# Second block of an attention and mixture-of-experts kernel: where on SyncE's queue a visit's stores of w1's sums stand

## The chip, the core and the metric

One Trainium2 chip, one NeuronCore. The metric is the time of one execution in device microseconds, lower is better. TensorE (PE) multiplies, VectorE (DVE), ScalarE (ACT) and GpSimd (POOL) work on elements, SyncE (SP) issues most of the transfers between HBM and SBUF. Each engine takes its instructions in program order and waits on semaphores for what the others make.

## The reference

Attention by random features for 4 batches of 8 heads (576 positions, 64 wide, 128 features), then a dense mixture of four experts over the 2304 rows that it gives:

```python
def phi(x):
    h = x @ omega.T - sum(x * x) / 2
    return exp(h - max(h)) / sqrt(m)
kv = phi(k).T @ v;  z = sum(phi(k))
x = (phi(q) @ kv) / (phi(q) @ z + 1e-6)          # 2304 x 512
p = domain_probs / domain_probs.sum(-1)
for e in range(4):                               # w1[e] 512 x 1024, w2[e] 1024 x 512
    out += p[:, e:e+1] * (relu(x @ w1[e]) @ w2[e])
```

## The kernel before

Every float32 operand of a matmul is split into a high and a low part of the type fp32r (`split`: ACT writes the high part at line 553, POOL mostly the low one at line 556), and a product is three matmuls. The rows are worked off in blocks. A *visit* is one block with one half of one expert's hidden layer. Visits 0 to N0-1 use plain products. The second block (u = 1, 768 rows) has eight visits, called visit 1 to visit 8 below, and the third (u = 2, 1024 rows) eight more. Both use a fast scheme with seven products of sums of the parts of x and of w1. For each visit, `sides` makes the parts and sums of w1: for each of two halves i (called half 0 and half 1) four tiles, `w1ah` and `w1al` (384 KB each) and `w1sh` and `w1sl` (512 KB each). There are two buffers of each of the four, so half 0 of the next visit goes to the buffer that half 0 of this visit holds. The second block makes the tiles; `keep_sides` also stores them to HBM (`kept`, line 661, eight transfers a visit on SP's queue), and the third block fetches them from there on POOL's queue.

In a visit `fast` writes the order out by hand. g is the half of w1 that a product uses, so `p1(0)` is product 1 with half 0. `keep` copies a product from PSUM to SBUF on ACT (line 928), `both` adds a product and a kept one on DVE (line 934), then relu on ACT (line 943) and the low part on DVE (line 947). Product 7 adds to the same PSUM bank that product 6 left (`start=False`), so `p7(1)` follows ACT's copy in `p6(1)`. `prepare()` stands four times in a visit of the second block (behind `p1(0)`, `p5(0)`, `p7(0)` and `p4(0)`), and each time splits one tile of w2 and then issues one load of w2 (line 549). There are three raw buffers (`w2r`), and a load takes the one that was just split, so the load behind the first split of a visit brings what the fourth split of the same visit reads. The other three bring tiles for the next visit. In the text they are load a, b, c and d. Behind `p6(1)`, `next(ready)` begins the next visit's `sides` with the split of w1 into `w1ah` and `w1al`; its steps end in the outputs, and each of its two `summed` steps issues one load of w1 (`w1r`). `begun(t)` begins an output tile (lines 744 to 746) with the first two hidden tiles. Loads of attention's k, q and v stand between visits.

```python
        p4(0)
        ...
        prepare()                  # fourth split of w2, load d
        ...
        p6(1)                      # product, then ACT's copy out of PSUM
        if v + 1 != DEEP[0]:
            next(ready, None)      # next visit: w1ah, w1al of half 0
        begun(0)
        p7(1)                      # adds to p6(1)'s bank
        begun(1)
        p3(1)
        p4(1)
        next(more, None)
        begun(2)
```

Of the kernel before, what the change touches and what calls it, by code (L numbers as in the profile page):

```python
# [6 lines left out]
F32 = mybir.dt.float32  # L7
# [7 lines left out]
def attention_moe(ctx, tc, kT, qT, kd, qd, kn, qn, vn, omT, probs, w1, w2, out):  # L15
# [10 lines left out]
    nc = tc.nc  # L26
# [4 lines left out]
    E, FP, P, _ = w1.shape  # L31
# [13 lines left out]
    scratch = ctx.enter_context(tc.tile_pool(name="scratch", bufs=1, space=bass.MemoryType.DRAM))  # L45
# [23 lines left out]
    def f32(ap):  # L69
        return ap.bitcast(F32)  # L70
# [32 lines left out]
    H = 2 * P  # L103
# [415 lines left out]
    def visit(u, n, c0, m):  # L519
        return (u, *HALVES[n], c0, m)  # L520

    BIG = {1: (START, 6 * P), 2: (START + 6 * P, 8 * P)}
    visits = [visit(0, n, 0, 2 * P) for n in range(3)]
# [63 lines left out]
    def split_w2():  # L587
        if not later_w2:
            return
        v, c = later_w2.pop(0)  # L590
        W[v, "w2", c] = a, b = pair_of(("w2h", 512), ("w2l", 512))
        split(raw.pop((v, "w2", c)), a, b, nc.scalar, nc.gpsimd)
        load("w2")
# [57 lines left out]

    made, kept = {}, {}

    def keep_sides(v):

        for i in range(2):
            kept[visits[v][1:3], i] = ts_ = tuple(
                scratch.tile([P, w * H], F32, tag=f"s{visits[v][1:3]}{i}{x}{w}", name="kept", bufs=1) for w in (3, 4) for x in "hl"
            )
            for k, t in zip(ts_, made.pop((v, i))):  # L660
                nc.sync.dma_start(k, f32(t))

    def sides(v):

# [218 lines left out]
    def fast(v):  # L883

        u, _, _, _, n = visits[v]
# [18 lines left out]
        def prepare():  # L904
            if deep:
                for _ in range(steps2.pop(0)):
                    next(ready2, None)
            else:
                split_w2()
# [4 lines left out]
        def product(g, p, where, start=True):  # L914
            if start:
                P_[g][where] = bank("g1")[:, :n]
            ps = P_[g][where]
            (wa, wc), (xa, xc) = W[v, "w1", g][p], X[p]
            for k in range(2):
                w = slice(k * P, (k + 1) * P)  # L920
                for a, x, at in ((wa, xa, 0), (wa, xc, 1), (wc, xa, 2)):
                    nc.tensor.matmul(  # L922
                        ps, a[:, w], x[:, k], start=(start and k + at == 0), stop=(k == 1 and at == 2), skip_group_check=not start
                    )

        def keep(g, where, name):
            P_[g][name] = t = held([P, 512], "sum", F32)[:, :n]
            nc.scalar.activation(t, P_[g][where], AF.Copy)  # L928
# [23 lines left out]
        def p1(g):  # L952
            product(g, 1, "u")
            keep(g, "u", "p1")
# [7 lines left out]
        def p5(g):  # L962
            product(g, 5, "b5")
            keep(g, "b5", "p5")
# [9 lines left out]
        def p4(g):  # L974
            product(g, 4, "u", start=False)
            ha, hc = (x[:, :n] for x in hs[2 * g + 1])
            nc.scalar.activation(ha, P_[g]["u"], AF.Relu)
            if deep and g == 0:
                nc.scalar.activation(r11[:, 1], P_[0]["u"], AF.Relu)
            nc.vector.scalar_tensor_tensor(hc, P_[g]["u"], 0.0, f32(ha), ALU.max, ALU.subtract)  # L980

        def p3(g):
            product(g, 3, "b5", start=False)
            both(g, 0, 1, "b5", "u2")
# [14 lines left out]
        def sevens():  # L999
# [88 lines left out]
                gathered(v, t)  # L1088
            yield 1

        p1(0)
        prepare()
        p2(0)
        if deep:
            prepare()
        p5(0)
        next(more, None)
        prepare()
# [18 lines left out]
            if v > DEEP[0] and v + 1 in DEEP:  # L1117
                start_sides2(v + 1)
        p3(0)
        if u == 1:  # L1120
            keep_sides(v)
        p4(0)
        if deep:
            less(t1[:, 1], P_[0]["p5"], r11[:, 1])
# [242 lines left out]
    def emit():  # L1367
        pairs, g1 = begin()
        later = [Halves(b, hp) for b in range(1, B) for hp in range(NP)]
        windows = {  # L1370
            0: (first_rest(pairs, opening(later[0], both=True)), 15 / 11),
            3: (joint_ticks(later[:-NP]), 76 / 45.4),
            N0: (chain(opening(later[-NP]), later_ticks(later[-NP:])), 54 / (NV * (BIG[1][1] // P + 1) * 0.8)),
        }
        ticks, n, done, per = iter(()), 0, 0.0, 0
        for v in range(len(visits)):
            if v in windows:
                for _ in ticks:
                    pass
                ticks, per = windows[v]  # L1380
                n, done = 0, 0.0
            for share in first_visit(g1) if v == 0 else fast(v) if v >= N0 else plain(v):
                done += share
                while n < done * per:
                    next(ticks, None)
                    n += 1
        store(0)
# [61 lines left out]
```

## Time and profile before

| | |
|---|---|
| median of 3 runs | 888.4 us (886.48 to 890.8) |
| the profiled execution | 886.87 us, its span 885.1 us |
| PE busy | 878.3 us, 99% of the span |
| granted TensorE clock | 1.000 of full speed, mean over the span |
| DVE, ACT, POOL busy | 586.4, 469.1, 564.7 us |
| SP's hardware queue | 102.95 MB, 35.2% of 16 engines' span |
| second block, visits 1 to 8 | from 283.7 us to about 566 us of the span |

The profile is of one execution. A busy PE is one with a matmul in flight; the waits that it lists are those in which nothing was in flight. The idle time of an engine other than PE costs nothing by itself.

### The profile page before, as it was taken

The numbers are of one execution on the slowest core, as the hardware profiler recorded it, in microseconds if no ns is written. First come the engines' busy times: TensorE is split into PE (matmuls) and PEld (weight loads), VectorE is DVE, ScalarE is ACT, GpSimd is POOL, SyncE is SP. The second block draws the span as 40 slices with busy tenths as digits, with TensorE's granted clock in tenths as the row PEclk, the third lists the DMA queues.
The fourth block names the chain that finished last, engine by engine and source line by source line (L and its number), as shares of the span: only waits on it lengthen the run. The fifth ranks groups of instructions, "written<-read, shape, count | busy, mean of one in ns | idle before, by whom it ended". The sixth has DMA issues, their size and how long they took to land.

```text
span 885.1 us, 14800 instructions
## 1 busy us (share of the span) xinstructions
PE 878.3 (99%) x5484; PEld 788.6 (89%) x5484; DVE 586.4 (66%) x1025; ACT 469.1 (53%) x1039; POOL 564.7 (64%) x494
## 2 busy tenths in 40 slices
PE   9999999999999999999999999999999999999998
PEld 9988888989888898988988899898989898998988
DVE  5755566666667646577675666975848476675847
ACT  6554677776774564555555544634443525444342
POOL 6656465555644455444454436779898888989874
PEclk9999999999999999999999999999999999999999
DMA  7664355434521856635466253834152442415132
GB/s 185 164 229 152 111 161 176 128 137 139 184 72 48 296 171 220 230 131 202 131 221 220 78 202 129 303 105 168 47 179 85 151 153 77 156 60 179 48 132 96
DMA packets 64552, 134.01 MB, mean 151 GB/s; under 512 B 10624, under 2 KB 21056, under 8 KB 64480
## 3 DMA queue, kind: packets, MB, share of 16 engines
q1 hardware_dynamic: 54512, 102.95, 35.2%
q0 software_dynamic: 9360, 29.82, 10.3%
q8 instruction: 43, 0.70, 0.3%
q10 hardware_dynamic: 608, 0.30, 0.1%
q14 instruction: 29, 0.24, 0.1%
HBM read 98.96 MB, written 34.08 MB: 150 GB/s over the span
## 4 chain that ended last, share of the span: by engine, by line
PE 89%; POOL 4%; DVE 2%; DMA 2%; issue 2%; ACT 1%; SPq 0%; POOLq 0%; ACTq 0%
PE g L922 26%; PE g L997 16%; PE g L744 8%; PE g L746 8%; PE g L745 8%; PE g L729 3%; PE g L730 3%; PE g L731 3%; PE kv L317 2%; PE k_ps L266 1%; PE q_ps L266 1%; PE qt_ps L328 1%; DMA kept<-w1ah 1%; PE q_ps L147 1%; PE kv L177 1%
## 5 line engine op out<-in xcount | busy, mean ns | idle before, releaser
L556 POOL TENSOR_TENSOR w2l<-w2r,w2h 128x512 fp32r<-128x512 f32 x93 | 123.8, 1337 | 85.4 <-ACT w2h L553 73.2
L773 DVE SCALAR_TENSOR_TENSOR acc<-g,pr,acc 128x256 f32<-128x256 f32 (+1 forms) x278 | 139.3, 539 | 37.7 <-PE g L746 27.8
L556 POOL TENSOR_TENSOR w1sl<-w1r,w1sh 128x512 fp32r<-128x512 f32 (+1 forms) x43 | 75.1, 1747 | 65.5 <-ACT w1sh L553 54.6
L744 PE MATMUL g<-w2h,hh 128*128 128x512 f32 x280 | 111.9, 400 | 1.5 <-DVE sum L934 1.3
L746 PE MATMUL g<-w2h,hl 128*128 128x512 f32 x280 | 109.7, 392 | 0.0
L745 PE MATMUL g<-w2l,hh 128*128 128x512 f32 x280 | 109.5, 391 | 0.0
L947 DVE SCALAR_TENSOR_TENSOR hl<-sum,hh 128x384 fp32r<-128x384 f32 (+1 forms) x64 | 46.8, 734 | 81.9 <-ACT hh L943 66.6
L934 DVE TENSOR_TENSOR sum<-g,sum 128x384 f32<-128x384 f32 (+1 forms) x96 | 59.3, 620 | 62.2 <-PE g L922 56.1
L922 PE MATMUL g<-xbh,w1sh 128*128 128x384 f32 (+1 forms) x256 | 93.1, 364 | 0.1
L922 PE MATMUL g<-xbl,w1sh 128*128 128x384 f32 (+1 forms) x256 | 92.9, 363 | 0.0
L922 PE MATMUL g<-xbh,w1sl 128*128 128x384 f32 (+1 forms) x256 | 92.6, 362 | 0.0
L556 POOL TENSOR_TENSOR w1al<-w1r,w1ah 128x512 fp32r<-128x512 f32 (+1 forms) x45 | 51.4, 1157 | 51.7 <-ACT w1ah L553 32.3
L928 ACT ACTIVATE sum<-g 128x384 f32<-128x384 f32 (+1 forms) x96 | 50.8, 540 | 51.5 <-PE g L922 50.4
L553 ACT ACTIVATE w2h<-w2r 128x512 fp32r<-128x512 f32 x90 | 55.3, 627 | 29.2 <-DMA w2r<-in_w 24.4
L922 PE MATMUL g<-xbh,w1ah 128*128 128x384 f32 (+1 forms) x192 | 70.1, 365 | 0.0
L922 PE MATMUL g<-xbl,w1ah 128*128 128x384 f32 (+1 forms) x192 | 69.6, 362 | 0.0
L922 PE MATMUL g<-xbh,w1al 128*128 128x384 f32 (+1 forms) x192 | 69.5, 362 | 0.0
L744 PEld LDWEIGHTS g<-w2h,hh 128*128 128x128 f32 x280 | 52.6, 188 | 12.2 <-DVE sum L934 1.6
L746 PEld LDWEIGHTS g<-w2h,hl 128*128 128x128 f32 x280 | 52.5, 188 | 11.8 <-DVE hl L980 0.5
L745 PEld LDWEIGHTS g<-w2l,hh 128*128 128x128 f32 x280 | 52.6, 188 | 9.0
L943 ACT ACTIVATE hh<-sum 128x384 fp32r<-128x384 f32 (+1 forms) x64 | 35.0, 549 | 42.3 <-DVE sum L934 41.9
L922 PEld LDWEIGHTS g<-xbh,w1sh 128*128 128x128 f32 x256 | 48.1, 188 | 6.2 <-DVE sum L934 0.6
(212 smaller groups left out, 2420.5 us busy)
## 6 DMA issues: line engine op xcount, KB each, us to landing
w2r<-in_w SPq DMA_DIRECT2D x108, 256.0 KB, 2.8
w1r<-in_w SPq DMA_DIRECT2D x38, 512.0 KB, 3.6
kept<-w1sh SPq DMA_DIRECT2D x16, 512.0 KB, 4.9
kept<-w1sl SPq DMA_DIRECT2D x16, 512.0 KB, 5.4
w1sh<-kept POOLq DMA_DIRECT2D x16, 512.0 KB, 6.0
w1sl<-kept POOLq DMA_DIRECT2D x16, 512.0 KB, 6.7
kept<-w1ah SPq DMA_DIRECT2D x16, 384.0 KB, 4.9
kept<-w1al SPq DMA_DIRECT2D x16, 384.0 KB, 4.9
```

Of the source, the lines that this page charges most:

```text
L553: hi.activation(a, t, AF.Copy)
L556: lo.tensor_tensor(c, t, f32(a), ALU.subtract)
L744: nc.tensor.matmul(ps, ha[:, ts_], wa, start=(c == 0), stop=False)
L745: nc.tensor.matmul(ps, ha[:, ts_], wc, start=False, stop=False)
L746: nc.tensor.matmul(ps, hc[:, ts_], wa, start=False, stop=(c == FH - 1))
L773: nc.vector.scalar_tensor_tensor(to, ps, sc, to, ALU.mult, ALU.add)
L922: nc.tensor.matmul(ps, a[:, w], x[:, k], start=(start and k + at == 0), stop=(k == 1 and at == 2), skip_group_check=not start)
L928: nc.scalar.activation(t, P_[g][where], AF.Copy)
L934: nc.vector.tensor_tensor(t, P_[g][where], t, ALU.add)
L943: nc.scalar.activation(ha, t, AF.Relu)
L947: nc.vector.scalar_tensor_tensor(x, y, 0.0, f32(z), ALU.max, ALU.subtract)
L997: nc.tensor.matmul(to, x, w, start=(start and f + k == 0), stop=(f + k == 3), skip_group_check=not start)
```

## The change

`keep_sides` takes the half as an argument, and is called twice in a visit of the second block: for half 0 in front of `p1(0)`, so its four stores stand on SP in front of load a, and for half 1 behind `p2(0)`, between load a and load b. Before, all eight stores stood behind `p3(0)`, between load c and load d. No transfer is added or taken away, and no other engine's instructions change their order.

```diff
-    def keep_sides(v):
-
-        for i in range(2):
-            kept[visits[v][1:3], i] = ts_ = tuple(
-                scratch.tile([P, w * H], F32, tag=f"s{visits[v][1:3]}{i}{x}{w}", name="kept", bufs=1) for w in (3, 4) for x in "hl"
-            )
-            for k, t in zip(ts_, made.pop((v, i))):
-                nc.sync.dma_start(k, f32(t))
+    def keep_sides(v, i):
+
+        kept[visits[v][1:3], i] = ts_ = tuple(
+            scratch.tile([P, w * H], F32, tag=f"s{visits[v][1:3]}{i}{x}{w}", name="kept", bufs=1) for w in (3, 4) for x in "hl"
+        )
+        for k, t in zip(ts_, made.pop((v, i))):
+            nc.sync.dma_start(k, f32(t))
...
+        if u == 1:
+            keep_sides(v, 0)
         p1(0)
         prepare()
         p2(0)
         if deep:
             prepare()
+        else:
+            keep_sides(v, 1)
         p5(0)
...
         p3(0)
-        if u == 1:
-            keep_sides(v)
         p4(0)
```

## Rows read from the trace of the kernel before

**Rows 1.** The page: busy time of the engines, the granted clock.
```profile
PE 878.3 (99%) x5484; PEld 788.6 (89%) x5484; DVE 586.4 (66%) x1025; ACT 469.1 (53%) x1039; POOL 564.7 (64%) x494
...
PEclk9999999999999999999999999999999999999999
```

**Rows 2.** Waits of PE: us in total, times, longest us.
```profile
PE g L744 <- DVE sum L934: 1.3, 1, 1.3
...
PE g L744 <- ACT kp L299: 0.2, 1, 0.2
```

**Rows 3.** Waits of all engines: those on the stores of `w1ah`.
```profile
ACT w1ah L553 <- DMA kept<-w1ah: 17.4, 9, 3.4
```

**Rows 4.** The chain in order of time, visit 6: start us, us, what.
```profile
476.09 4.86 DMA kept<-w1ah
...
481.05 0.94 ACT w1ah L553 x2
...
482.44 1.35 DVE hl L947
...
484.31 0.50 PE g L744
```

**Rows 5.** Timeline of SP, 364.6 to 372.5, visit 3: start us, us.
```profile
364.78 0.42 SPq L661 DMA_DIRECT2D kept<-w1ah  x1
...
371.14 1.12 SPq L661 DMA_DIRECT2D kept<-w1sl  x1
372.35 1.05 SPq L549 DMA_DIRECT2D w2r<-in_w  x1
```

**Rows 6.** The eight stores of rows 5 alone.
```profile
DMA to landing us min/median/max: 3.5/4.9/5.4
```

**Rows 7.** The load of rows 5, issued at 372.35, alone.
```profile
DMA to landing us min/median/max: 4.8/4.8/4.8
```

**Rows 8.** Timeline of SP, 288 to 291, visit 1.
```profile
288.13 0.34 SPq L549 DMA_DIRECT2D w1r<-in_w  x1
288.52 1.42 SPq L792 DMA_DIRECT2D out<-acc  x2
290.10 0.37 SPq L549 DMA_DIRECT2D w2r<-in_w  x1
```

**Rows 9.** The load of w2 issued at 290.10 alone.
```profile
DMA to landing us min/median/max: 4.1/4.1/4.1
```

**Rows 10.** Timelines of ACT and PE, visit 1.
```profile
295.20 0.62 ACT L553 ACTIVATE w2h<-w2r 128x512 fp32r<-128x512 f32 x1
295.72 0.48 ACT L928 ACTIVATE sum<-g 128x384 f32<-128x384 f32 x1
...
296.52 0.34 PE L922 MATMUL g<-xbh,w1sh 128*128 128x384 f32 x1
```

**Rows 11.** Timelines of SP, ACT and PE, visit 4.
```profile
394.98 0.33 SPq L549 DMA_DIRECT2D w2r<-in_w  x1
...
402.97 0.49 ACT L928 ACTIVATE sum<-g 128x384 f32<-128x384 f32 x1
...
404.10 0.33 PE L922 MATMUL g<-xbh,w1sh 128*128 128x384 f32 x1
```

**Rows 12.** The load of w2 issued at 394.98 alone.
```profile
DMA to landing us min/median/max: 4.0/4.0/4.0
```

**Rows 13.** Timelines of SP and PE, visit 2.
```profile
318.05 0.33 SPq L549 DMA_DIRECT2D w1r<-in_w  x1
...
329.29 0.33 PE L922 MATMUL g<-xbh,w1sh 128*128 128x384 f32 x1
```

**Rows 14.** The load of w1 issued at 318.05 alone.
```profile
DMA to landing us min/median/max: 3.5/3.5/3.5
```

**Rows 15.** Timeline of POOL, 547 to 556, visit 8.
```profile
548.97 0.73 POOL L606 TENSOR_TENSOR va<-w2r 128x256 f32<-128x256 f32 x1 [0.46 <-DMA w2r<-in_w]
...
554.15 2.35 POOL L556 TENSOR_TENSOR w2s<-va,w2s 128x512 fp32r<-128x512 f32 x1 [1.81 <-ACT w2s L553]
```

**Rows 16.** The eight stores of visit 1 alone, issued from 295.6 to 303.
```profile
DMA to landing us min/median/max: 3.4/5.9/6.3
```

## The prediction, made before the change was run

> **What bounds the kernel now.** I read the page first. TensorE is busy in 99% of the span, at its full granted clock (2.4 GHz) in all 40 slices, and no other engine is above two thirds [rows 1]. So a wait counts only if TensorE stands still for it. The list of TensorE's own waits says how much of that there is: one wait of 1.3 us on VectorE's sum and one of 0.2 us on ScalarE's kp are the only ones in the second block [rows 2]. The list over all engines then shows what the stores cost today: ScalarE waits 17.4 us in nine waits, the longest 3.4 us, before it may overwrite `w1ah`, because the store out of that buffer has not landed [rows 3]. The chain in order of time ties one of these waits to TensorE. In visit 6 the store of `w1ah` takes 4.9 us, ScalarE's split follows at 481.05, its relu is queued behind, then VectorE's low part, then its sum, and the output matmul at 484.31 is the one that lost 1.3 us [rows 2, 4]. The shorter one, in visit 3, stands behind such a wait too. So of 17.4 us of waiting TensorE felt 1.5 us.
>
> **What the change takes away.** Half 0 is stored in front of `p1(0)`, nine products earlier, and needs no new producer: its tiles were split during the visit before. At `next(ready)` its stores have then landed, and ScalarE goes straight on. The most that this can give is what TensorE lost: 1.3 + 0.2 = 1.5 us [rows 2]. The rest of the 17.4 us lies beside matmuls, and is worth nothing. Stores and attention's loads behind load d also come earlier; TensorE has no wait of its own on them, so nothing there either.
>
> **What it adds: four stores in front of load a.** No instruction is added; eight transfers change their place in SP's queue. Half 0 brings 2 x 384 + 2 x 512 = 1792 KB ahead of load a, whose 256 KB the fourth split of the same visit reads. The price of such a queue is shown in visit 3: the first of eight stores lands at 364.8 + 3.5 = 368.3, the last at 371.1 + 5.4 = 376.5, so the other seven (3200 KB) take 8.2 us, 390 KB a microsecond [rows 5, 6]. Four stores then cost 1792 / 390 = 4.6 us, and a load of 256 KB 0.7 us. The load behind those eight landed at 372.4 + 4.8 = 377.2, 0.7 us after the last store [rows 5, 7]: a load does not pass the stores ahead of it. So where the queue is busy when the visit begins, load a lands 4.6 us later than now.
>
> The Trainium skill, "DMA: Bandwidth & Descriptors", section "Where 436 GB/s comes from", gives a ceiling of 435 GB/s; by it the same stores would take an estimated 4.2 us, and the sum below would come out 0.8 us lower. No run here shows a queue of stores at that ceiling; I keep the row's 4.6.
>
> **Who waits for load a.** The fourth split is in front of `p6(1)`'s copy on ScalarE, and `p7(1)` adds to the bank that this copy reads. A late load a thus stops ScalarE at the split, behind it the copy, and behind that TensorE at `p7(1)`, with only the six matmuls of `begun(0)` between. In visit 1 split and copy take from 295.20 to 296.20, and `p7(1)` starts at 296.52 [rows 10]. From landing to `p7(1)` I take 1.0 for split and copy and 0.1 for the hand-overs: 1.1 us. Load a may then land 1.1 us before `p7(1)`'s present start at the latest.
>
> Visit 1: the load of w1 and two stores of finished outputs are in the queue just before (288.13, 288.52), and load a, issued at 290.10, lands at 294.2 [rows 8, 9]. The limit is 295.4. With four stores ahead it lands at 298.8, `p7(1)` starts at 299.9, and TensorE loses 299.9 - 296.5 = **3.4 us**.
>
> Visit 4: attention's loads are ahead of it; load a lands at 395.0 + 4.0 = 399.0 [rows 11, 12]. Then 399.0 + 4.6 = 403.6, `p7(1)` at 404.7 instead of 404.1: **0.6 us**.
>
> Visit 2, the tightest of the rest: the load of w1 ahead lands at 318.1 + 3.5 = 321.6, then the stores, then load a: 321.6 + 4.6 + 0.7 = 326.9, against a limit of 329.3 - 1.1 = 328.2 [rows 13, 14]. It has 1.3 us to spare, and loses nothing. Visits 3 and 5 to 8 have more.
>
> **Half 1 and the other loads.** Its four stores now stand ahead of loads b, c and d. Those bring tiles that the next visit splits, over 10 us later; a delay of 4.6 us is hidden by the visit's outputs. The exception is visit 8, where loads b and c feed GpSimd's sums at 548.97, which already wait 0.5 us; c would land about 2 us later. GpSimd then idles 1.8 us before its next split [rows 15], so I cost this at nothing, and at up to 2 us with that cover gone. The second overwriting, of half 1's `w1ah`, comes in the outputs, after its stores have had their 4.6 us. GpSimd issues no transfer in this block before visit 8's end, so its queue is passed by nothing.
>
> **The sum**, in microseconds: + 3.4 (visit 1) + 0.6 (visit 4) - 1.5 (waits removed) + 0 (the rest) = **+2.5**. The profiled execution took 886.9, so it becomes 889.4. The median of the runs shown is 1.5 above that execution, 888.4, and my forecast stands against the median: 888.4 + 2.5 = **890.9**. Bounds: load a not held up at all gives -1.5. Upwards, the eight stores of visit 1 need up to 6.3 us from issue to landing where those of visit 3 need 5.4 [rows 6, 16]; if all of these 0.9 us fell on four stores, visits 1 and 4 would lose 0.9 more each: +4.3.
>
> That is within 0.5% (4.4 us), about what a measurement of this kernel can tell from no change.
>
> **Rivals.**
> 1. *Load a is not late* (chance 0.20): load and stores go side by side, or the stores leave before the queue is full. For it: load a is small and reads, the stores write. Against it: the load behind eight stores came out after them [rows 5 to 7]. Then only the gain is left: 888.4 - 1.5 = 886.9.
> 2. *Slower by more than 0.5%* (0.13): one mechanism, the same late load a in visits 1 and 4, with a slower queue. It decides when four stores take 5.6 us: visits 1 and 4 each lose 1.0 more, and 2.5 + 2 x 1.0 is over 4.4. Visit 2 joins at 4.6 + 1.3 = 5.9 us. At 7 us it is 3.4 + 0.6 + 2 x 2.4 + 1.1 (visit 2) - 1.5 = +8.4, or 896.8. For it: stores and the load of w1 overlap at the visit's start, which today they do not. Against: 390 KB a microsecond held over eight stores [rows 5, 6], and even the slower eight of visit 1 stay under that point [rows 16].
> 3. *The pause costs clock* (0.07): all slices show full clock, and the longest pause in them is 1.3 us [rows 1, 2]; 3.4 us in visit 1 would be new. If matmuls then ran at 1.2 GHz for as long as the pause, they would do half the work in it: 1.7 us more, 888.4 + 2.5 + 1.7 = 892.6. The Trainium skill, "TensorE: Matmul & The Clock Gate", section "HAM oscillation — how this bites in real kernels", warns of such pauses; no row of this trace has a fall to show.
> 4. *The change does not do what it says* (0.05): ScalarE's overwriting waits as long, for the matmuls that read the same buffer. No gain and the loss of visits 1 and 4: 888.4 + 4.0 = 892.4.
>
> The forecast itself has 0.55, with 889.2 to 892.3 as its own range.
>
> **The numbers.** Over 0.5% slower (above 892.8): rival 2, half of rivals 3 and 4, and a little of the forecast's upper end by the runs' own spread, 0.2 in all. Over 0.5% faster (below 884.0): no case reaches it, 0.03 for what I have not seen. The rest, 0.77, is the same. The range goes from rival 1's value to past rivals 3 and 4, with about a microsecond of the runs' spread on the low side: 885.9 to 894.2.
>
> **What would show it.** Right: ScalarE's waits on the stores are gone from the list; TensorE's 1.3 us in visit 6 too; a wait of about 3 us stands in visit 1 at line 922, `p7(1)`, with ScalarE waiting for `w2r` at 295; a smaller one in visit 4. Wrong: load a of visit 1 lands before 296, or TensorE gets waits at the first split of a visit, by load b, which I called hidden, or on VectorE in the third block.

## The result and the profile after

The changed kernel takes 895.67 us (median of 6 runs, 893.64 to 897.02), the kernel before 889.29 us (6 runs beside them). The ratio is 1.0072, with a 95% interval of 1.0051 to 1.0093: 6.4 us slower. The forecast was 890.9 with a range up to 894.2, so the time lies above the range: a loss of 2.5 us was forecast, and it is 6.4 us.

The profiled execution took 897.02 us. Its page answers to [rows 1]:

```profile
span 895.2 us, 14800 instructions
...
PE 881.7 (98%) x5484; PEld 791.1 (88%) x5484; DVE 587.5 (66%) x1025; ACT 469.6 (52%) x1039; POOL 563.7 (63%) x494
...
PEclk9999999999999899999999999999999999999999
```

One slice of the granted clock is no longer full. The list of TensorE's waits answers to [rows 2] (us in total, times, longest us):

```profile
PE g L921 <- ACT sum L927: 6.2, 3, 3.1
...
PE g L921 <- DVE sum L933: 0.9, 1, 0.9
PE q_ps L266 <- DVE qtl L339: 0.9, 1, 0.9
```

The 1.3 us of visit 6 are gone, and with them every wait of ScalarE on the stores that [rows 3] showed. In their place stand three waits for ScalarE's copy, 6.2 us. To see where they lie, I took each visit's length from the timeline: from the first matmul of `p1(0)` to that of the next visit (the changed kernel's visit 1 runs from 285.00 to 323.48, so 38.48). All profiled executions of this study, in microseconds; a visit that lost time against the kernel before by over 0.4 us is marked:

| kernel | visit 1 | visit 2 | visit 3 | visit 4 | visit 6 | first of third block |
|---|---|---|---|---|---|---|
| before | 32.76 | 37.44 | 37.29 | 36.22 | 37.74 | 39.02 |
| changed | **38.48** | **40.01** | 36.69 | **37.32** | 36.15 | **40.16** |
| e1, visit 1 as before | 32.79 | **37.88** | 36.69 | **37.28** | 36.15 | **39.77** |
| e2, visit 1 alone changed | **37.11** | **41.55** | 37.44 | 36.22 | 37.35 | 39.00 |
| e3, half 0 behind load a | 32.55 | **41.40** | 36.69 | 36.22 | 36.13 | **42.22** |
| e4, changed, pause filled | **35.83** | **40.01** | 36.69 | **37.79** | 36.15 | **40.07** |
| e5, e3 with k last | **33.83** | 37.44 | 36.69 | 36.22 | 36.15 | **42.01** |
| e6, changed with k last | **37.61** | **41.61** | 36.69 | **37.51** | 36.15 | **39.79** |
| e7, before with k early | **36.49** | **41.48** | 37.34 | 36.22 | 37.33 | 39.01 |
| e8, visits 2 to 7 only | 32.88 | 37.44 | 36.69 | 36.22 | 36.13 | 39.01 |
| e9, e3 with visit 8 as before | 32.55 | **40.01** | 36.69 | 36.22 | 36.13 | 39.00 |

Visits 5, 7 and 8 differ by at most 0.2 us between all of these. The changed kernel's row against the first: + 5.7 + 2.6 - 0.6 + 1.1 - 1.6 + 1.1 = +8.3. The spans differ by 10.1; of the rest 1.3 came before the second block, where nothing was changed, and 0.5 in later visits of the third block.

**Visit 1: the late load, and the clock behind it.** The timelines of SP, ScalarE and TensorE in the changed kernel:

```profile
289.84 1.43 SPq L791 DMA_DIRECT2D out<-acc  x2
291.32 0.47 SPq L660 DMA_DIRECT2D kept<-w1ah  x1
...
293.65 1.06 SPq L660 DMA_DIRECT2D kept<-w1sl  x1
294.80 1.07 SPq L549 DMA_DIRECT2D w2r<-in_w  x1
...
300.02 0.63 ACT L553 ACTIVATE w2h<-w2r 128x512 fp32r<-128x512 f32 x1 [3.39 <-DMA w2r<-in_w]
300.55 0.47 ACT L927 ACTIVATE sum<-g 128x384 f32<-128x384 f32 x1
...
301.08 0.69 PE L921 MATMUL g<-xbh,w1sh 128*128 128x384 f32 x1 [3.05 <-ACT sum L927]
```

This is the chain that was forecast: four stores, load a behind them, the fourth split of w2 on ScalarE, the copy, and `p7(1)`, where TensorE stood still for 3.05 us (forecast: 3.4). Load a landed at 294.80 + 5.2 = 300.0, 15.0 us behind the visit's start, and in the kernel before 10.5 us behind it (294.2 - 283.7): 4.5 us later, where 4.6 were forecast. What was not in the sum is the clock behind the pause. The windows of the changed kernel (start and end, then busy time of each engine, then the granted clock):

```profile
296.00:300.00 4.00, 2.02 (x10) 1.41 (x8) 1.17 (x2) 0.63 (x2) 0.57 (x1) 1.00 1.02 409
300.00:306.80 6.80, 5.72 (x16) 5.17 (x17) 1.12 (x2) 2.36 (x5) 3.19 (x3) 0.50 1.01 361
306.80:312.00 5.20, 5.20 (x27) 4.54 (x26) 3.19 (x7) 1.68 (x4) 0.00 (x0) 1.00 0.83 281
```

From 300.0 to 306.8 the clock granted was 0.50, 1.2 GHz of 2.4. TensorE got through 16 matmuls in 6.8 us, and through 27 in the next 5.2.

**Visit 4** has the same wait at `p7(1)`, shorter and without a fall of the clock:

```profile
414.11 0.44 PE L921 MATMUL g<-xbh,w1sh 128*128 128x384 f32 x1 [0.83 <-ACT sum L927]
```

**Visit 2: VectorE held up by GpSimd.** TensorE's second wait is in front of `p6(0)`, at 329.07, for 2.28 us: ScalarE's copy of `p1(0)` was late, behind exponentials that waited for VectorE's `nbk` (their bias):

```profile
325.13 0.74 ACT L306 ACTIVATE kp<-t_ps,nbk 64x128 f32<-64x128 f32 x2 [2.53 <-DVE nbk L293]
...
328.47 0.55 ACT L927 ACTIVATE sum<-g 128x384 f32<-128x384 f32 x1
...
329.07 0.44 PE L921 MATMUL g<-xbh,w1sh 128*128 128x384 f32 x1 [2.28 <-ACT sum L927]
```

VectorE and GpSimd in the changed kernel, some 10 us before:

```profile
314.57 1.35 DVE L674 TENSOR_TENSOR w1r<-w1r 128x256 f32<-128x256 f32 x1 [3.23 <-POOL w1al L556]
315.96 2.48 DVE L675 TENSOR_TENSOR w1r<-w1r 128x256 f32<-128x256 f32 x1
318.47 1.25 DVE L676 TENSOR_TENSOR w1r<-w1r 128x256 f32<-128x256 f32 x1
...
320.10 0.75 DVE L255 TENSOR_REDUCE sqk<-k 128x9 f32<-128x576 f32 x1
...
322.80 2.30 DVE L293 SCALAR_TENSOR_TENSOR nbk<-sqk,mxk 128x9 f32<-128x9 f32 x1
...
314.49 1.16 POOL L251 TENSOR_TENSOR k<-k 128x576 f32<-128x576 f32 x1
315.70 2.46 POOL L556 TENSOR_TENSOR w1sl<-w1r,w1sh 128x1024 fp32r<-128x1024 f32 x1
318.12 1.33 POOL L251 TENSOR_TENSOR q<-q 128x576 f32<-128x576 f32 x1
322.68 2.40 POOL L556 TENSOR_TENSOR w1sl<-w1r,w1sh 128x1024 fp32r<-128x1024 f32 x1 [3.23 <-ACT w1sh L553]
```

Each of these three sums of VectorE ends just after a GpSimd instruction ends (315.92 and 315.65, 318.44 and 318.16, 319.72 and 319.45), and `nbk`, 9 columns wide, takes 2.30 us under a split of 2.40. The same place in the kernel before:

```profile
307.82 0.42 DVE L675 TENSOR_TENSOR w1r<-w1r 128x256 f32<-128x256 f32 x1 [2.26 <-POOL w1al L556]
...
311.39 0.76 DVE L255 TENSOR_REDUCE sqk<-k 128x9 f32<-128x576 f32 x1 [1.77 <-POOL k L251]
...
314.88 0.17 DVE L293 SCALAR_TENSOR_TENSOR nbk<-sqk,mxk 128x9 f32<-128x9 f32 x1
...
310.21 1.15 POOL L251 TENSOR_TENSOR k<-k 128x576 f32<-128x576 f32 x1 [2.42 <-DMA q<-in_qd]
311.32 2.39 POOL L556 TENSOR_TENSOR w1sl<-w1r,w1sh 128x1024 fp32r<-128x1024 f32 x1
...
315.63 2.40 POOL L556 TENSOR_TENSOR w1sl<-w1r,w1sh 128x1024 fp32r<-128x1024 f32 x1 [0.81 <-ACT w1sh L553]
```

There a sum took 0.42 us, because GpSimd stood idle for 2.42 us: attention's load, behind eight stores, had not landed (the row names a transfer of q; k's second one landed at 310.14). And `nbk` was done at 315.05, before GpSimd's second split began at 315.63. Counted from the start of visit 2 (316.43 before, 323.48 changed), the sums made VectorE 1.7 us late; that brought `nbk` under the split, where it took 2.1 us more. An instruction between them was 0.8 us quicker, so `nbk` ended 3.0 us later. The waiting that looked idle had kept the two engines apart.

**Third block.** GpSimd's first sum of w2, [rows 15], waits eight times as long in the changed kernel:

```profile
560.80 0.73 POOL L606 TENSOR_TENSOR va<-w2r 128x256 f32<-128x256 f32 x1 [3.75 <-DMA w2r<-in_w]
```

### The profile page after: what moved, and what is told of

Read it like the earlier page. It is cut to its first block, busy times and chain, and to the rows that moved or that the text cites. A ratio compares the mean times of both kernels' runs of the same rounds, so it can differ in the third digit from the quotient of the medians.

```text
span 895.2 us, 14800 instructions
## 1 busy us (share of the span) xinstructions
PE 881.7 (98%) x5484; PEld 791.1 (88%) x5484; DVE 587.5 (66%) x1025; ACT 469.6 (52%) x1039; POOL 563.7 (63%) x494
## 4 chain that ended last, share of the span: by engine, by line
PE 85%; DVE 8%; issue 2%; ACT 1%; DMA 1%; POOL 1%; SPq 0%; ACTq 0%; POOLq 0%; DVEq 0%
PE g L921 26%; PE g L996 17%; PE g L743 6%; PE g L744 6%; PE g L745 6%; PE g L728 3%; PE g L729 3%; PE g L730 3%; PE kv L317 2%; DVE xbl L556 2%; DMA w2r<-in_w 1%; PE q_ps L266 1%; PE k_ps L266 1%; DVE acc L772 1%; PE qt_ps L328 1%
## 5 line engine op out<-in xcount | busy, mean ns | idle before, releaser
L946 DVE SCALAR_TENSOR_TENSOR hl<-sum,hh 128x384 fp32r<-128x384 f32 (+1 forms) x64 | 41.0, 643 | 75.7 <-ACT hh L942 55.8
L556 POOL TENSOR_TENSOR w1al<-w1r,w1ah 128x512 fp32r<-128x512 f32 (+1 forms) x45 | 49.2, 1108 | 49.1 <-ACT w1ah L553 40.6
L743 PEld LDWEIGHTS g<-w2h,hh 128*128 128x128 f32 x280 | 52.9, 189 | 10.5 <-DVE hl L735 0.4
```

Source lines behind the costliest of these rows:

```text
L556: lo.tensor_tensor(c, t, f32(a), ALU.subtract)
L743: nc.tensor.matmul(ps, ha[:, ts_], wa, start=(c == 0), stop=False)
L946: nc.vector.scalar_tensor_tensor(x, y, 0.0, f32(z), ALU.max, ALU.subtract)
```

## The experiments

Ratios are to runs of the kernel before on the same chip, with 95% intervals.

**e1, visit 1 as before.**

```diff
-        if u == 1:
+        if u == 1 and v != N0:
             keep_sides(v, 0)
...
-        else:
+        elif v != N0:
             keep_sides(v, 1)
...
         p3(0)
+        if u == 1 and v == N0:
+            for i in range(2):
+                keep_sides(v, i)
```

> Visit 1 alone has its eight stores back behind p3(0); visits 2 to 8 stay as changed. My theory: in visit 1 the stores of half 0 hold load a up, TensorE pauses at p7(1) (3.1 us) and its clock then falls to half for 6.8 us, some 6.6 us together, and the 2.3 us wait of visit 2 comes out of visit 1 too, since attention's loads are no longer held back by its stores. So both go, what stays is 1.0 in visit 4 and the 1.3 to 1.5 us gained in visit 6: within 1 us of the kernel before, ratio 0.998 to 1.001. Rival, the stores' traffic beside a visit's first products costs time in every visit: seven of eight visits still have it, so about +5.5 us, ratio 1.006.

Measured: 889.35 us, ratio 1.0013 (0.9999 to 1.0028). Most of the loss comes with visit 1's stores; the rival, a cost of each visit's traffic, is out. Visits 1 and 2 are back to within 0.1 and 0.4 us, visit 4 keeps its 1.1.

**e2, only visit 1 changed.** The conditions of e1 the other way round (`v == N0` at the first two, `v != N0` at the third).

> Only visit 1 is changed; visits 2 to 8 have their stores behind p3(0) as before. My theory: the pause and the half clock in visit 1 and the wait in visit 2 are all there, without visit 4's 1.0 and without the gain in visit 6: 7 to 9 us over the kernel before, ratio 1.008 to 1.010. Rival, a cost of each visit's traffic: an eighth of the change's 6.4, under 1 us, ratio 1.001.

Measured: 896.97 us, ratio 1.0100 (1.0079 to 1.0122). By the medians one visit of eight costs more than the whole change, though the two intervals overlap. The gains of visits 3 and 6 are missing here, but so are the losses of visit 4 and of the third block, about 2 us each way. What is left points to the clock: in the profiled execution it fell twice, and the mean clock of all six runs is 0.994 to 0.996, where four of the changed kernel's six have 0.998. The windows show the two falls, behind the pause of visit 1 and behind the wait in visit 2:

```profile
300.70:304.10 3.40, 2.95 (x9) 2.75 (x10) 0.56 (x1) 1.25 (x5) 3.20 (x3) 0.50 1.02 391
...
328.00:331.40 3.40, 3.40 (x11) 3.40 (x12) 0.44 (x1) 1.76 (x4) 2.53 (x2) 0.50 0.20 34
```

**e3, half 0 behind load a in all visits.**

```diff
-        if u == 1:
-            keep_sides(v, 0)
         p1(0)
         prepare()
+        if u == 1:
+            keep_sides(v, 0)
         p2(0)
```

> In all eight visits half 0's stores stand behind load a instead of in front of it, half 1's stay behind p2(0). My theory: load a lands in time, so the pause and the half clock of visit 1 and the 1.0 of visit 4 go, and the gain in visit 6 stays. What it tells is the 2.3 us of visit 2: if they come from attention's loads being earlier (GpSimd then works while VectorE makes sums of w1, and VectorE is slowed), they stay, and the time is 0.5 to 1.5 us over the kernel before, ratio 1.001. If they are only an after-effect of visit 1's pause, they go, 1.5 us under it, ratio 0.998. Rival, traffic: still some 6 us over, ratio 1.007.

Measured: 891.69 us, ratio 1.0035 (1.0019 to 1.0051). The pauses of visits 1 and 4 are gone (32.55 and 36.22), so load a behind the stores is their cause. Visit 2's wait is still there without a pause in visit 1, so it is no after-effect; VectorE's sums meet GpSimd's work on k here too:

```profile
308.25 1.36 DVE L675 TENSOR_TENSOR w1r<-w1r 128x256 f32<-128x256 f32 x1
309.64 2.48 DVE L676 TENSOR_TENSOR w1r<-w1r 128x256 f32<-128x256 f32 x1
312.16 1.25 DVE L677 TENSOR_TENSOR w1r<-w1r 128x256 f32<-128x256 f32 x1
...
308.18 1.15 POOL L251 TENSOR_TENSOR k<-k 128x576 f32<-128x576 f32 x1 [0.42 <-DMA k<-in_kn]
```

A loss that I had not expected came in: the first visit of the third block takes 42.22 us.

**e4, the pause of visit 1 filled.** Twelve matmuls into the bank of `begun(1)`, which `begun(1)` then overwrites:

```diff
         def begun(t):
-            g2[t] = bank("g2")
+            if t not in g2:
+                g2[t] = bank("g2")
...
         begun(0)
+        if v == N0:
+            g2[1] = bank("g2")
+            for _ in range(12):
+                nc.tensor.matmul(g2[1], hs[0][0][:, :P], W[v, "w2", 0][0], start=True, stop=True)
         p7(1)
         begun(1)
```

> The changed kernel with twelve idle matmuls (their bank is overwritten afterwards) between begun(0) and p7(1) of visit 1, 12 x 0.227 = 2.7 us of work laid into the pause. Load a lands as late as in the changed kernel, so p7(1) starts as late. If the half clock behind the pause costs by itself, as my theory has it, the clock stays at full and visit 1 is about 3.4 us shorter than in the changed kernel: 3 us over the kernel before, ratio 1.003. If the half clock costs nothing, the time is that of the changed kernel, ratio 1.007; if the pause is not a wait for load a, the matmuls add 2.7 us to it, ratio 1.010.

Measured: 894.68 us, ratio 1.0070 (1.0051 to 1.0089), not the 3 us less that I expected. In the profile the filling did what it was to do: `p7(1)` starts as late, the clock stays full, and visit 1 is 35.83 instead of 38.48 us.

```profile
300.00:306.80 6.80, 6.80 (x35) 6.10 (x34) 4.10 (x8) 1.91 (x5) 2.61 (x3) 1.00 0.98 348
```

So 6.8 us at half clock cost 2.65 us, and e2's 3.4 us in visit 1 cost 37.11 - 35.83 = 1.3 us. But the changed kernel's profiled execution, with the lowest mean clock of its six runs (0.995, four others have 0.998), had the long fall. The mean clock of two of e4's runs is 1.000, and they took 894.64 and 895.03 us. The usual run of the changed kernel, at 0.998, has by its mean clock room for one short fall, 1.3 us or so, which is less than these runs can tell.

**e5, e3 with k loaded last.** In visit 1, where the first pair of the next attention part is loaded (a flag of `opening` takes this order there alone, and the old one elsewhere):

```diff
-        p.load("k")
+        p.load_v()
+        p.load_tails()
         yield
         p.load("q")
         yield
-        p.load_v()
-        p.load_tails()
+        p.load("k")
         yield
```

> The kernel with half 0 behind load a, and in visit 1 the loads of the first pair of that attention part turned round: v and its tails first, then q, then k (k was first). No store moves, and GpSimd's and VectorE's orders stay. In the kernel with half 0 behind load a, k landed at 308.1, GpSimd squared it at once while VectorE made the second sums of w1, and VectorE's four sums took 5.6 us instead of 1.8. My theory: with k last it lands 2 to 3 us later, about 310.8, as it did behind the stores; the sums are over by then, the 2.4 us wait of visit 2 goes and its half clock with it: 3 to 4 us under the kernel with half 0 behind load a, ratio to the kernel before 0.997 to 1.000. Rival: the wait comes from the split into w1ah that no longer waits for the stores; this is unchanged here, so the wait stays and the ratio is 1.0035.

Measured: 889.33 us, ratio 1.0017 (1.0001 to 1.0032). This is 0.0018 under e3, some 1.6 us, and the two intervals overlap; what shows the part of k is the profile. No store moved, and visit 2 fell from 41.40 to 37.44, to the hundredth that of the kernel before. The timelines of e5 show why, and also the price of a late k:

```profile
308.42 0.43 DVE L683 TENSOR_TENSOR w1r<-w1r 128x256 f32<-128x256 f32 x1 [3.22 <-POOL w1al L565]
...
309.80 0.43 DVE L686 TENSOR_TENSOR w1r<-w1r 128x256 f32<-128x256 f32 x1
...
312.44 1.15 POOL L251 TENSOR_TENSOR k<-k 128x576 f32<-128x576 f32 x1 [4.05 <-DMA k<-in_kn]
...
311.69 0.38 PE L266 MATMUL k_ps<-om_r,k 64*128 64x128 f32 x2 [1.18 <-DMA k<-in_kd]
```

All four sums take 0.42 to 0.43 us again. TensorE itself waits 1.18 us for k in visit 1; the third block keeps its loss.

**e6, the changed kernel with k last.** The edit of e5 on the changed kernel.

> The changed kernel with the same three loads of visit 1 turned round, k last. My theory: visit 1's pause and half clock stay (visit 1 about 37 to 38.5 us instead of 32.8), visit 2's wait of 2.4 us goes; 2.4 to 3.5 us under the changed kernel, ratio 1.004. Rival as above: 1.007.

Measured: 897.30 us, ratio 1.0097 (1.0069 to 1.0124). My expectation failed. The pause in visit 1 delays VectorE's sums by more than the turned order delays k: GpSimd was held by its split until 313.1, k had landed by then, and the collision stayed.

```profile
313.15 1.35 DVE L683 TENSOR_TENSOR w1r<-w1r 128x256 f32<-128x256 f32 x1 [3.23 <-POOL w1al L565]
...
313.07 1.16 POOL L251 TENSOR_TENSOR k<-k 128x576 f32<-128x576 f32 x1
```

**e7, the kernel before with k early.** The load of k of that pair in front of visit 1's eight stores (`opening` leaves its own load of k out there):

```diff
         p3(0)
+        if v == N0:
+            soon[0].load("k")
         if u == 1:
             keep_sides(v)
```

> The kernel before, all stores in their old place behind p3(0), with one thing moved: in visit 1 the load of k of the first pair (two transfers) stands in front of the eight stores instead of behind them and load d. My theory: k is there early, GpSimd's square and split run against VectorE's second sums of w1, and visit 2 gets the 2.4 us wait that the kernel before does not have: 2.4 to 4 us slower, ratio 1.003 to 1.004. Rival (the wait comes from the split into w1ah that no longer waits for stores): that split still waits here, by 1.5 us longer, and visit 2 is as before, ratio 1.000 to 1.001.

Measured: 895.16 us, ratio 1.0075 (1.0047 to 1.0103), twice the upper end of what I expected. Visit 2 has the wait and the half clock (41.48), although the split into `w1ah` waited longer for the stores than in the kernel before, 6.39 us; so the rival is out. The other half is a wait in visit 1: the stores, two transfers later, held that split, behind it the relu, and TensorE for 3.37 us.

```profile
304.24 0.94 ACT L554 ACTIVATE w1ah<-w1r 128x512 fp32r<-128x512 f32 x2 [6.39 <-DMA kept<-w1ah]
...
308.36 0.50 PE L745 MATMUL g<-w2h,hh 128*128 128x512 f32 x1 [3.37 <-ACT hh L978]
```

As this pause also delayed VectorE's sums, e7 alone does not isolate the early k; e3 against e5 does.

**e8, visits 2 to 7 only.** Order of e3 in visits 2 to 7; visits 1 and 8 have all eight stores behind `p3(0)`, with conditions on `v` as in e1.

> Visits 2 to 7 have half 0 behind load a and half 1 behind p2(0); visits 1 and 8 have all eight stores behind p3(0) as before. My theory: no load a is late, attention's loads of visit 1 stay behind its stores, loads b and c of visit 8 stay ahead of its stores; what is left is the gain: 0.6 in visit 3 and 1.6 in visit 6, 2.2 us under the kernel before, ratio 0.997 to 0.998. If moving the stores costs anything in a visit by itself, the ratio is 1.000 or above.

Measured: 885.88 us (11 runs) beside 887.42 us (21 runs), ratio 0.9983 (0.9974 to 0.9992): 1.5 us faster than the kernel before, and the fastest here. TensorE has no wait left in the second block; the whole list is

```profile
PE warm L1179 <- DVE om_r L1170: 1.1, 1, 1.1
PE q_ps L266 <- DVE qtl L339: 0.7, 1, 0.7
PE g L996 <- DVE hl L979: 0.6, 2, 0.4
```

**e9, e3 with visit 8 as before.**

> The kernel with half 0 behind load a in all visits, but visit 8 has its stores behind p3(0) as before. My theory: loads b and c of visit 8 no longer stand behind its stores, GpSimd's sums for the third block start 5 us earlier than in that kernel, and the first visit of the third block shrinks from 42.2 back to 39.0 us; visit 2's wait stays. 3 us under that kernel: ratio to the kernel before 1.000 to 1.002. Rival, that the first visit of the third block varies by itself from run to run: it stays about 42 us, ratio 1.0035.

Measured: 889.00 us, ratio 1.0016 (1.0004 to 1.0027), 0.0019 under e3 or some 1.7 us, where I expected 3. The first visit of the third block is back at 39.00 us. GpSimd's first sum in e3, and then in e9:

```profile
558.53 1.79 POOL L606 TENSOR_TENSOR va<-w2r 128x256 f32<-128x256 f32 x1 [8.01 <-DMA w2r<-in_w]
```

```profile
549.60 0.74 POOL L606 TENSOR_TENSOR va<-w2r 128x256 f32<-128x256 f32 x1 [0.38 <-DMA w2r<-in_w]
```

e9 and e8 differ in visit 1's stores alone, and were measured beside the same runs of the kernel before: 889.00 and 885.88 us, with intervals that do not touch. So moving the stores of visit 1 costs 3.1 us even where load a is not late, and the loss in the profile is visit 2's wait (40.01 against 37.44 us).

## Why the prediction was wrong, step by step

1. *The gain of at most 1.5 us.* Right in kind: ScalarE's waits on the stores went, and visits 3 and 6 are 0.6 and 1.6 us shorter, 2.2 together. Visit 3 gave 0.4 and visit 6 0.3 us more than the waits listed for them, so the list was no upper bound. Other visits with a single wait show the same: visit 4 lost 1.10 us with 0.83 listed, e1's visit 2 0.44 with 0.15. The list counts only the time with no matmul in flight, while in a stream without waits a matmul of 128x384 starts every 0.17 us and is in flight for 0.33, so 0.16 us of each wait stay uncounted; the matmul behind the first also starts 0.1 us late (329.35 behind 329.07). A listed wait thus costs some 0.3 us more than it says. What is left of visit 3 I did not follow.
2. *Load a behind four stores, 3.4 us in visit 1 and 0.6 in visit 4, nothing in visit 2.* Right: 3.05 and 0.83 us of waiting; e2 and e3 show the cause. For visit 2 the forecast was nothing; e1, where visit 1 does not disturb it, has 0.4 us there.
3. *"Stores and attention's loads behind load d also come earlier; TensorE has no wait of its own on them, so nothing there either."* This is the step that failed: a term put at nothing that measured 2.6 us. The wait that these loads caused before was GpSimd's, and it kept GpSimd's square and split out of VectorE's way. With the loads earlier, three sums took 1.25 to 2.48 us instead of 0.42, `nbk` behind them 2.30 instead of 0.17, and TensorE lost 2.6 us in visit 2. e3 against e5 shows it in the profile: same stores, k later, and the loss is gone. The Trainium skill, "SBUF — State Buffer", section "Who interferes with whom", states that a VectorE instruction with two inputs in SBUF contends with a GpSimd instruction that reads there; the durations here agree, 0.42 us alone and up to 2.48 beside GpSimd. I had not held that rule against the moved work.
4. *The half clock as a rival with a chance of 0.07.* I held it for another outcome, but it is a term that comes on top of the forecast's own pause: every profiled execution with a pause of about 3 us in visit 1 left unfilled at `p7(1)` shows it (changed, e2, e6). The 3.37 us of e7, at another place of visit 1, did not bring it. It came behind the 2.3 us wait of visit 2 as well in e2, e3, e6 and e7, and there not in the changed kernel, e4 and e9; I priced one of them at 1.7 us, and 3.4 us at half clock cost 1.3 to 1.6. The Trainium skill, "TensorE: Matmul & The Clock Gate", section "HAM oscillation — how this bites in real kernels", describes a kernel whose TensorE waits some 3 to 5 us for a transfer between groups of matmuls and then starts at the low clock. The trace agrees, with 0.50 granted behind 3.05 us of standing still, but not in every case, as e7 shows.
5. *Loads b and c of visit 8, "at nothing, and at up to 2 us with that cover gone".* The cover was too short. GpSimd waited 3.75 us instead of 0.5 for load c, which landed 3.3 us later in the visit where I took 2, and the 1.8 us of idle time in front of its next split were used up. The third block's first visit took 1.1 us more, and TensorE's one wait there, 0.9 us, is the wait on VectorE in the third block that the prediction named as a sign of being wrong. With all eight stores between load a and load b (e3) the loss is 3.2, and e9 takes it back. There TensorE's first wait is 0.9 us for a fetch of `w1sl`, which GpSimd issues behind those sums; the prediction left these fetches out, though they begin at 556.5 in the kernel before, 10 us ahead of visit 8's end. How the changed kernel's late sums lead to its 0.9 us on VectorE was not followed step by step.

With the terms as they were in the profile, visit by visit: 5.7 (3.1 pause, 2.6 clock) + 2.6 + 1.1 + 1.1 - 2.2 = +8.3, the same sum as from the table; with a shorter fall of the clock, 1.3 instead of 2.6, it is +7.0, beside +6.4 measured over the runs' medians.

Open: e7's two waits are not told apart in its time, and how the half clock is shared over unprofiled runs is only seen in their mean clock.

## What to carry to other kernels

A transfer moved forward in a queue moves every transfer behind it back, and every one that it stood in front of forward; both lists have to be followed to who reads them, and a load that the same stage reads must stay ahead of stores that nobody waits for. An engine's idle time off the critical path can be what keeps it off a resource that the next engine needs: before removing a wait, look at what then runs at the same time. A forecast pause of TensorE of some three microseconds is to be priced with what its clock does afterwards.

## What the runs showed of the hardware

A `scalar_tensor_tensor` of 9 columns on VectorE took 0.17 us alone and 2.30 us beside a GpSimd split of 128x1024, ending 0.02 us after it. A `tensor_reduce` of 128x576, which reads one tensor, took 0.75 us alone (320.10 in the changed kernel) and 0.76 beside such a split (311.39 in the kernel before). TensorE's granted clock fell to 0.50 at waits as short as 2.3 us, for 3.4 us, in some executions of kernels with the same wait and not in others (visit 2: 41.40 us in e3, 40.01 in e9).
